# A fused attention and two-block kernel: the last block's first product as seven block products for two tiles of tokens at once

## The chip, the core and the metric

One core of a Trainium2 chip runs the whole program in one launch. The metric is the time of one execution on the device in microseconds (us). The chip's engines are named as in the profile: PE is TensorE's matmuls, PEld its weight loads, DVE is VectorE, ACT is ScalarE, POOL is GpSimd, SP is SyncE, which here only issues transfers.

## What is computed

Attention with pooled keys and values feeds a block that routes each token to one of eight experts, and a second, dense block follows. The change touches only the dense block:

```python
def _moe2_ref(x, w_in, w_out, g_ln):          # x: 4608 x 512, w_in: 512 x 1024, w_out: 1024 x 512
    h = x @ w_in
    e = np.exp(h - np.max(h, axis=-1, keepdims=True))
    solu = h * (e / (np.sum(e, axis=-1, keepdims=True) + 1e-09))
    mu = np.mean(solu, axis=-1, keepdims=True)
    var = np.mean((solu - mu) ** 2, axis=-1, keepdims=True)
    return ((solu - mu) / np.sqrt(var + 1e-06) * g_ln) @ w_out
```

## The kernel before

Tokens are worked on in 36 tiles of 128. Every float32 matrix product is done in float16 with each operand split into a high and a low part (the low part is what is left after rounding): high by high, high by low and low by high, so three matmuls for each 128 rows of the contraction. The split of a 128-row tile is a ScalarE copy into float16 (high) and a VectorE scalar_tensor_tensor (low, L119, L843, L849, L874, L1213). The tile of tokens is TensorE's stationary operand, so it must lie transposed; a DMA transpose issued by SyncE does that, in blocks of 128 x 128.

The program is ordered by hand: each engine's queue holds its instructions in the order in which the Python code emits them, and an instruction that waits holds up all that stand behind it on its engine.

The expert block runs expert by expert in eight tiles each (`body`). Weights of later stages are loaded, decoded and split between its groups of matmuls; lists called `works` hold these steps, and `body` takes one after each of its four groups of matmuls and one in the middle of the second product, and what is left over at its end, ahead of `fin`, which adds the tile's result and scatters it to `xres` with a GpSimd transfer. `d_load`, `d_decode`, `d_split` do that for `w_in` (i = 0 to 3) and `w_out` (4 to 7), in experts 5, 6 and 7 (`DP`). In the last expert `m_load` and `m_xt` also load, split and transpose the first three tiles of the dense block.

The dense block is the loop at the end. For tile i: `m_h` makes the first product in two halves of 512 columns, 12 matmuls each (L1159), and a maximum of each half (L1164). `m_soft` makes the exponential on ScalarE (L1181), the product with it and its sum on VectorE (L1185), and the sum of squares on ScalarE (L1188). `m_var` makes the reciprocal root: a power on GpSimd (L1198) between small VectorE operations. `m_norm` normalises on VectorE (L1207), splits (L1211, L1213) and transposes (L1212, L1214). `m_out` is the second product, 24 matmuls (L1222), its eviction on ScalarE (L1225) and the store (L1226). The order within the loop:

```python
for i in range(NT + AHEAD):          # AHEAD = 3: m_out runs three tiles behind m_h
    m_load(i + 4); m_h(i, 0)
    m_xt(i + 3)                      # the input of the tile three ahead
    m_h(i, 1); m_soft(i)
    m_norm(i - 1)
    m_var(i)
    m_out(i - AHEAD)
```

(the conditions at the first and last tiles are left out here). The halves have three PSUM banks each, the second product two.

## Time and profile before

| | |
|---|---|
| Median of three runs | 983.17 us (981.6 to 995.12) |
| The profiled execution, its own time | 977.48 us |
| Its span in the profile | 975.8 us |
| TensorE, mean granted clock over the span | 0.952 of full speed |
| Busy: PE, DVE, ACT, POOL | 891.2, 626.8, 429.8, 297.9 us |
| Matmuls | 7,838 |

The profile is one execution recorded by the hardware. A busy engine is one with an instruction in it; matmuls are pipelined, so a matmul's row shows 379 ns while the next one starts 216 ns later. The chain of work is followed back from the last instruction, at each step to what released it. The stage windows give the busy time of every engine in a stretch of the span, and beside it the clock that TensorE was granted (1.00 is 2.4 GHz, 0.50 is 1.2 GHz) and the mean busy share of the 16 DMA engines.

### The profile page before, as it was taken

The page shows a single profiled execution, that of the slowest core. Times are in us where ns is not written, and L with a number is a line of the kernel's source. Part 1 is how long each engine was busy: PE and PEld are TensorE (multiplying, and loading weights), DVE is VectorE, ACT ScalarE, POOL GpSimd, SP SyncE. Part 2 cuts the span into 40 slices and gives each one's busy share as a digit, 9 for nine tenths or more (in the row PEclk, how much of TensorE's full clock was granted, in tenths as well). Part 3 has the DMA queues.
Part 4 walks back from the last instruction along what each step waited for, and adds up shares of the span by engine and source line. Part 5 has one row for each costly group of instructions (what it writes and reads, how often), then busy time and mean ns, then how long its engine had stood idle before and what let it go on. Part 6 is the DMA issues. An engine that isn't in the chain of part 4 may idle for free. (4 is left out here: it accounts for less than half of the span.)

```text
span 975.8 us, 20287 instructions
## 1 busy us (share of the span) xinstructions
PE 891.2 (91%) x7838; PEld 563.5 (58%) x7838; DVE 626.8 (64%) x1420; ACT 429.8 (44%) x1002; POOL 297.9 (31%) x255
## 2 busy tenths in 40 slices
...
GB/s 292 226 344 336 229 265 269 108 214 186 338 156 228 183 186 184 241 236 69 82 120 171 98 55 56 104 127 148 142 128 161 110 125 145 109 136 134 98 98 86
DMA packets 189309, 163.98 MB, mean 168 GB/s; under 512 B 137296, under 2 KB 145488, under 8 KB 188656
## 3 DMA queue, kind: packets, MB, share of 16 engines
...
q14 instruction: 61, 0.50, 0.2%
...
## 5 line engine op out<-in xcount | busy, mean ns | idle before, releaser
L1222 PE MATMUL po<-woh,zt 128*128 128x512 f16 x576 | 177.9, 381 | 2.0 <-ACT o L1225 2.0
L1159 PE MATMUL ph<-wih,xt 128*128 128x512 f16 x576 | 176.7, 379 | 1.0 <-DVEq L1130 1.0
L1222 PEld LDWEIGHTS <-zt 128*128 128x128 f16 x864 | 84.9, 98 | 105.4 <-issue 4.6
L1159 PEld LDWEIGHTS <-xt 128*128 128x128 f16 x864 | 84.5, 98 | 103.2 <-issue 1.5
L1198 POOL TENSOR_TENSOR rr<-va,mhalf 128x1 f32<-128x1 f32 x36 | 19.8, 550 | 343.1 <-DVE va L1197 343.1
L1181 ACT ACTIVATE wst<-ph,ng 128x512 f32<-128x512 f32 x72 | 48.9, 683 | 158.4 <-DVE ng L1177 146.2
L1222 PE MATMUL po<-wol,zt 128*128 128x512 f16 x288 | 109.8, 381 | 0.0
L1159 PE MATMUL ph<-wil,xt 128*128 128x512 f16 x288 | 109.2, 379 | 0.0
L938 PE MATMUL ph<-xt,wsb 128*128 128x128 f16 x1536 | 93.5, 223 | 9.9 <-PEq L1136 8.8
L942 ACT ACTIVATE hh<-ph 128x256 f16<-128x256 f32 x104 | 38.5, 381 | 144.3 <-PE ph L938 133.6
L938 PEld LDWEIGHTS <-wsb 128*128 128x128 f16 x1536 | 91.0, 100 | 15.4 <-issue 12.8
L950 PE MATMUL py<-wsb,hh 128*128 128x512 f16 x256 | 76.2, 379 | 0.5 <-ACT hh L942 0.5
L943 DVE SCALAR_TENSOR_TENSOR hl<-ph,hh 128x256 f16<-128x256 f32 x104 | 42.5, 419 | 48.8 <-ACT hh L942 47.9
L1213 DVE SCALAR_TENSOR_TENSOR zl<-wst,zh 128x1024 f16<-128x1024 f32 x36 | 44.1, 1225 | 45.3 <-ACT zh L1211 45.3
L938 PE MATMUL ph<-xt,wsa 128*128 128x128 f16 x960 | 60.8, 226 | 12.5 <-PEq L1136 7.1
L1185 DVE SCALAR_TENSOR_TENSOR wst<-ph,wst 128x512 f32<-128x512 f32 x72 | 49.0, 692 | 30.6 <-ACT wst L1181 30.6
...
L938 PEld LDWEIGHTS <-wsa 128*128 128x128 f16 x960 | 58.4, 102 | 16.4 <-issue 13.2
L505 PE MATMUL px<-vbh,ah 128*128 128x148 f16 (+1 forms) x320 | 51.6, 228 | 16.3 <-DVE lraw L538 11.6
L269 POOL TENSOR_TENSOR kv<-kv 128x1280 f32<-128x1280 f32 (+3 forms) x28 | 57.7, 2060 | 22.3 <-DMA kv<-in_k_dram 21.1
L950 PEld LDWEIGHTS <-hh 128*128 128x128 f16 x416 | 39.3, 99 | 42.4 <-ACT hh L942 1.8
L1164 DVE TENSOR_REDUCE mx<-ph 128x1 f32<-128x512 f32 x72 | 49.4, 686 | 21.0 <-PE ph L1159 20.9
...
## 6 DMA issues: line engine op xcount, KB each, us to landing
...
```

Source lines behind the costliest of these rows:

```text
L269: eng.tensor_tensor(x_[:, :, 0:r, :], x_[:, :, 0:r, :], x_[:, :, r:2 * r, :], ALU.add)
L505: T.matmul(hd[sl, a, h:h + x1 - x0, :], s_, w_[rw, c0 + x0:c0 + x1, :], start=(n == 0 and bl == 2 * a), stop=(n == 2 and bl == 2 * a + 2))
L938: T.matmul(o_, ww[:, kc * DF + fc * P:kc * DF + (fc + 1) * P], xt[s_][:, x0 + kc, :], start=(n == 0), stop=(n == 11))
L942: S.activation(hh[hb][:, sl], ph, AF.Relu)
L943: V.scalar_tensor_tensor(hl[hb][:, sl], ph, 0.0, hh[hb][:, sl], ALU.max, ALU.subtract)
L950: T.matmul(py[hb], xx[:, fc * P:(fc + 1) * P], ww[:, fc * DM:(fc + 1) * DM], start=(fc == 0 and n == 0), stop=(fc == NFC - 1 and n == 2))
L1159: T.matmul(ph, xt[:, xx, :], ww[:, ws], start=(n == 0), stop=(n == 11))
L1164: V.tensor_reduce(sx[i]["mx"][:, half:half + 1], ph, axis=AX.X, op=ALU.max)
L1181: S.activation(e_[:, o_], ph[a], AF.Exp, bias=ng, scale=CE, accum_out=s2[:, a:a + 1])
L1185: V.scalar_tensor_tensor(u_[:, o_], ph[a], 1.0, e_[:, o_], ALU.mult, ALU.mult, accum_out=su[:, a:a + 1])
L1213: V.scalar_tensor_tensor(zl, u_, SZ, zh, ALU.mult, ALU.subtract)
L1222: T.matmul(po, zt[:, xx, :], ww[:, ws], start=(fc == 0 and n == 0), stop=(fc == NFC - 1 and n == 2))
```

## The change

Two tiles of tokens, a and b, make a pair. Their rows of x are taken as a 2 by 2 block matrix (tile a and b by the left and right 256 columns), `w_in` as another (256 rows by 512 columns each), and the product's four blocks come from seven block products of 128 x 256 by 256 x 512, six matmuls each, in Strassen's form with few additions. The sums of the blocks of x (`m_sum`, four per pair) and of the weight (`b_sum`, four in all) are made on GpSimd, the seven additions of products on VectorE, one product is copied out by ScalarE (`c1`). `m_xt` splits and transposes 1,536 columns of x and 2,048 of sums for a pair, in two DMA transposes. Products 1 and 7 share one PSUM bank, each of the other five has one of its own. The result h now lies in SBUF, so that exponential, product and maximum are each one operation of 1,024 columns. `m_var` is wholly on GpSimd (seven operations of 128 x 1), and the normalisation moves from VectorE to ScalarE. `m_soft` is split: what follows the exponential (`m_solu`) runs in the next pair's iteration. The second product runs two pairs behind, in quarters between the seven products. Only pair 0 is loaded in the last expert; pair 1 is loaded, summed, split and transposed ahead of the loop, later ones inside the loop of the pair before. The decoded `w_in` stays in `raw` and is split as seven blocks in the last expert.

```diff
--- before.py
+++ after.py
 NTAB = 4
 LATE = 26
 NTL = 3
-AHEAD = 3
-NPRE = 3
+AHEAD = 2
...
-    wih, wil, woh, wol = (dp.tile([P, 4096], F16, name=n) for n in ("wih", "wil", "woh", "wol"))
+    woh, wol = (dp.tile([P, 4096], F16, name=n) for n in ("woh", "wol"))
+    raw = dp.tile([P, 4, 1024], I32, name="raw")
...
+    def d_steps(i):
+        return d_decode(i) + ([] if i < 4 else [lambda: d_split(i)]) + [lambda: d_next(i)]
...
+    NB = ("11", "21", "22", "T1", "T2", "T3", "T4")
+    def wblk(n, lo):
+        k_ = NB.index(n) + 7 * lo
+        return wset[0][k_ // 4][:, (k_ % 4) * 1024:(k_ % 4 + 1) * 1024].rearrange(
+            "p (c d) -> p c d", c=2)
...
+    rwf = raw.bitcast(F32)
+    bsrc = {f"{a + 1}{b + 1}": rwf[:, 2 * a:2 * a + 2, 512 * b:512 * b + 512]
+            for a in range(2) for b in range(2)}
+    for i in range(4):
+        bsrc[f"T{i + 1}"] = wst[4 + i].rearrange("p (c d) -> p c d", c=2)
+    def b_sum(n, x0, x1):
+        G.tensor_tensor(bsrc[n], bsrc[x0], bsrc[x1], ALU.subtract)
+    def b_split(n):
+        S.activation(wblk(n, 0), bsrc[n], AF.Copy, scale=SWI)
+        V.scalar_tensor_tensor(wblk(n, 1), bsrc[n], SWI, wblk(n, 0), ALU.mult, ALU.subtract)
+    b_steps = [lambda: b_sum("T1", "12", "11"), lambda: b_split("11"), lambda: b_split("21"),
+               lambda: b_sum("T2", "22", "T1"), lambda: b_split("22"), lambda: b_split("T1"),
+               lambda: b_sum("T3", "22", "12"), lambda: b_split("T2"),
+               lambda: b_sum("T4", "21", "T2"), lambda: b_split("T3"), lambda: b_split("T4")]
...
+    def m_load(j, a):
+        if j == 0:
+            t_ = xg[gset(E, a)]
+        else:
+            t_ = dst[j % 2].bitcast(F32)[:, a * DM:(a + 1) * DM]
+        (G if j == 0 else nc.sync).dma_start(t_, m_rows(xres[P:XROWS, :], 2 * j + a))
+        sx.setdefault(j, {})[a] = t_
+    def m_sum(j):
+        xa, xb = sx[j][0], sx[j][1]
+        l_, r_ = slice(0, 256), slice(256, 512)
+        s_ = wst[4 + j % 2].rearrange("p (k d) -> p k d", k=4)
+        G.tensor_tensor(s_[:, 0], xb[:, l_], xb[:, r_], ALU.add)
+        G.tensor_tensor(s_[:, 2], xa[:, l_], xb[:, l_], ALU.subtract)
+        G.tensor_tensor(s_[:, 1], s_[:, 0], xa[:, l_], ALU.subtract)
+        G.tensor_tensor(s_[:, 3], xa[:, r_], s_[:, 1], ALU.subtract)
+    def m_xt(j):
+        d = sx[j]
+        xa, xb = d[0], d[1]
+        if j == 0:
+            ha, hs, xta, xts = (wst[i].bitcast(F16) for i in range(4))
+        else:
+            h_, x_ = wset[1][2 + j % 2], wset[1][j % 2]
+            ha, hs, xta, xts = h_[:, 0:1536], h_[:, 2048:], x_[:, 0:1536], x_[:, 2048:]
+        ha, hs, xta, xts = ha[:, 0:1536], hs[:, 0:2048], xta[:, 0:1536], xts[:, 0:2048]
+        s_ = wst[4 + j % 2]
+        S.activation(ha[:, 0:512], xa, AF.Copy, scale=SX2)
+        V.scalar_tensor_tensor(ha[:, 768:1280], xa, SX2, ha[:, 0:512], ALU.mult, ALU.subtract)
+        S.activation(ha[:, 512:768], xb[:, 256:], AF.Copy, scale=SX2)
+        V.scalar_tensor_tensor(ha[:, 1280:], xb[:, 256:], SX2, ha[:, 512:768], ALU.mult,
+                               ALU.subtract)
+        S.activation(hs[:, 0:1024], s_, AF.Copy, scale=SX2)
+        V.scalar_tensor_tensor(hs[:, 1024:], s_, SX2, hs[:, 0:1024], ALU.mult, ALU.subtract)
+        xta, xts = (t_.rearrange("p (c t) -> p c t", t=P) for t_ in (xta, xts))
+        nc.sync.dma_start_transpose(xta, ha)
+        nc.sync.dma_start_transpose(xts, hs)
+        d["A"] = {n: (xta[:, 2 * k:2 * k + 2], xta[:, 6 + 2 * k:8 + 2 * k])
+                  for k, n in enumerate(("11", "12", "22"))}
+        d["A"] |= {f"S{k + 1}": (xts[:, 2 * k:2 * k + 2], xts[:, 8 + 2 * k:10 + 2 * k])
...
-        DP = {E - 3: (0, 1), E - 2: (2, 3), E - 1: (4, 5, 6, 7)}
+        DP = {E - 3: (0, 1), E - 2: (2, 3, 4), E - 1: (5, 6, 7)}
...
             for n, j in enumerate(DP.get(e, ())):
-                works[n if last else n + 1] += [lambda f_=f_, j=j: f_(j)
-                                                for f_ in (d_decode, d_split, d_next)]
+                works[n + 1] += d_steps(j)
+            if last:
+                works[0] += b_steps[:5]
+                works[1] += b_steps[5:]
...
             if last:
-                m_load(0)
-                works[1].append(lambda: m_xt(0))
-                for i in range(1, NPRE):
-                    works[min(i + 1, nstatic - 1)] += (
-                        [lambda i=i: m_load(i)] + 3 * [lambda: None] + [lambda i=i: m_xt(i)])
+                m_load(0, 0)
+                works[2] += [lambda: m_load(0, 1)]
+                works[3] += [lambda: m_sum(0), lambda: None, lambda: m_xt(0)]
...
-        def m_h(i, half):
...
-            ph = pp.tile([P, 512], F32, tag=f"ph2{half}", name=f"ph2{half}", bufs=AHEAD)
-            n = 0
-            for kc in range(NKC):
-                ws = slice(kc * DF + half * 512, kc * DF + half * 512 + 512)
-                for xx, ww in ((kc, wih), (kc, wil), (NKC + kc, wih)):
-                    T.matmul(ph, xt[:, xx, :], ww[:, ws], start=(n == 0), stop=(n == 11))
-                    n += 1
...
-            V.tensor_reduce(sx[i]["mx"][:, half:half + 1], ph, axis=AX.X, op=ALU.max)
+        MM = {1: ("11", "11"), 2: ("12", "21"), 3: ("S4", "22"), 4: ("22", "T4"), 5: ("S1", "T1"),
+              6: ("S2", "T2"), 7: ("S3", "T3")}
+        def m_p(j, n):
+            bank = pp.tile([P, 512], F32, tag=f"b{n % 6}", name=f"b{n % 6}")
+            a, b = MM[n]
+            ah, al = sx[j]["A"][a]
+            k_ = 0
+            for c in range(2):
+                for xx, lo in ((ah, 0), (ah, 1), (al, 0)):
+                    T.matmul(bank, xx[:, c, :], wblk(b, lo)[:, c, :], start=(k_ == 0), stop=(k_ == 5))
+                    k_ += 1
+            return bank
...
         def m_soft(i):
...
-            d = sx[i]
-            ph = (d.pop(0), d.pop(1))
+            d = sx[i // 2, i % 2]
             def sm(nm, w=1):
                 d[nm] = fp.tile([P, w], F32, tag=nm, name=nm)
                 return d[nm]
-            mx, ng, s2, su = d["mx"], sm("ng2"), sm("s2_", 2), sm("su2", 2)
-            nm_, s_ = sm("nm2"), sm("ss2")
-            V.tensor_scalar(ng, mx[:, 0:1], mx[:, 1:2], -CE, ALU.max, ALU.mult)
+            d["sm"] = sm
+            mx, ng, s2 = sm("mx2"), sm("ng2"), sm("s2_")
+            V.tensor_reduce(mx, d["h"], axis=AX.X, op=ALU.max)
+            V.tensor_scalar(ng, mx, -CE, None, ALU.mult)
+            S.activation(wst[i % 2], d["h"], AF.Exp, bias=ng, scale=CE, accum_out=s2)
+        def m_solu(i):
+            d = sx[i // 2, i % 2]
+            sm = d.pop("sm")
+            su, nm_, s_ = sm("su2"), sm("nm2"), sm("ss2")
             e_, u_ = wst[i % 2], wst[2 + i % 2]
-            for a in range(2):
-                o_ = slice(a * 512, a * 512 + 512)
-                S.activation(e_[:, o_], ph[a], AF.Exp, bias=ng, scale=CE,
-                             accum_out=s2[:, a:a + 1])
-            for a in range(2):
-                o_ = slice(a * 512, a * 512 + 512)
-                V.scalar_tensor_tensor(u_[:, o_], ph[a], 1.0, e_[:, o_], ALU.mult, ALU.mult,
-                                       accum_out=su[:, a:a + 1])
-            V.tensor_scalar(nm_, su[:, 0:1], su[:, 1:2], -1.0 / DF, ALU.add, ALU.mult)
+            V.scalar_tensor_tensor(u_, d.pop("h"), 1.0, e_, ALU.mult, ALU.mult, accum_out=su)
+            V.tensor_scalar(nm_, su, -1.0 / DF, None, ALU.mult)
             S.activation(e_, u_, AF.Square, bias=nm_, accum_out=sm("sv2"))
-            V.tensor_scalar(s_, s2[:, 0:1], s2[:, 1:2], 1e-9, ALU.add, ALU.add)
+            V.tensor_scalar(s_, d["s2_"], 1e-9, None, ALU.add)
             V.scalar_tensor_tensor(s_, s_, EPS, s_, ALU.mult, ALU.mult)
         def m_var(i):
-            d = sx[i]
-            v_, r_, t_ = (fp.tile([P, 1], F32, tag=nm, name=nm) for nm in ("va2", "rr2", "tt2"))
-            d["r"] = r_
-            V.scalar_tensor_tensor(v_, d["sv2"], 1.0 / DF, d["ss2"], ALU.mult, ALU.add)
+            d = sx[i // 2, i % 2]
+            v_, r_, t_, nr_ = (fp.tile([P, 1], F32, tag=nm, name=nm)
+                               for nm in ("va2", "rr2", "tt2", "nr2"))
+            d["r"], d["nr"] = r_, nr_
+            G.tensor_scalar(v_, d["sv2"], 1.0 / DF, d["ss2"], ALU.mult, ALU.add)
             G.tensor_tensor(r_, v_, mhalf, ALU.pow)
-            V.scalar_tensor_tensor(t_, r_, v_, r_, ALU.mult, ALU.mult)
-            V.tensor_scalar(t_, t_, -0.5, 1.5, ALU.mult, ALU.add)
-            V.tensor_tensor(r_, r_, t_, ALU.mult)
+            G.tensor_tensor(t_, r_, r_, ALU.mult)
+            G.tensor_tensor(t_, t_, v_, ALU.mult)
+            G.tensor_scalar(t_, t_, -0.5, 1.5, ALU.mult, ALU.add)
+            G.tensor_tensor(r_, r_, t_, ALU.mult)
+            G.tensor_tensor(nr_, r_, d["nm2"], ALU.mult)
         def m_norm(i):
-            d = sx[i]
+            d = sx[i // 2, i % 2]
             u_ = wst[2 + i % 2]
-            V.tensor_scalar(u_, u_, d["nm2"], d["r"], ALU.add, ALU.mult)
-            d["zt"] = zt = fp.tile([P, 2 * NFC, P], F16, tag="zt", name="zt", bufs=AHEAD + 1)
+            S.activation(u_, u_, AF.Identity, bias=d["nr"], scale=d["r"])
+            d["zt"] = zt = fp.tile([P, 2 * NFC, P], F16, tag="zt", name="zt", bufs=4)
             zh = fp.tile([P, DF], F16, tag="zh", name="zh")
             zl = fp.tile([P, DF], F16, tag="zl", name="zl")
             S.activation(zh, u_, AF.Copy, scale=SZ)
...
             V.scalar_tensor_tensor(zl, u_, SZ, zh, ALU.mult, ALU.subtract)
             nc.sync.dma_start_transpose(zt[:, NFC:], zl)
-        def m_out(i):
-            zt = sx.pop(i)["zt"]
-            po = pp.tile([P, 512], F32, tag="po", name="po", bufs=2)
-            for fc in range(NFC):
+        def m_out(i, part):
+            d = sx[i // 2, i % 2]
+            zt = d["zt"]
+            if part == 0:
+                d["po"] = pp.tile([P, 512], F32, tag="po", name="po", bufs=2)
+            po = d["po"]
+            for fc in range(4 * part, 4 * part + 4):
                 ws = slice(fc * DM, (fc + 1) * DM)
                 for n, (xx, ww) in enumerate(((fc, woh), (fc, wol), (NFC + fc, woh))):
                     T.matmul(po, zt[:, xx, :], ww[:, ws], start=(fc == 0 and n == 0),
                              stop=(fc == NFC - 1 and n == 2))
-            o_ = fp.tile([P, DM], F32, tag="o2", name="o2")
-            S.activation(o_, po, AF.Copy, scale=1.0 / (SZ * SWO))
-            nc.sync.dma_start(m_rows(out, i), o_)
+            if part == 1:
+                o_ = fp.tile([P, DM], F32, tag="o2", name="o2")
+                S.activation(o_, po, AF.Copy, scale=1.0 / (SZ * SWO))
+                nc.sync.dma_start(m_rows(out, i), o_)
...
-        for i in range(NPRE, 4):
-            m_load(i)
-        for i in range(NT + AHEAD):
-            if i + 4 < NT:
-                m_load(i + 4)
-            if i < NT:
-                m_h(i, 0)
-            if 1 <= i and i + 3 < NT:
-                m_xt(i + 3)
-            if i < NT:
-                m_h(i, 1)
-            if i < NT:
-                m_soft(i)
-            if i == 0:
-                m_xt(3)
-            if 4 <= i <= NT:
-                m_norm(i - 1)
-            if i < NT:
-                m_var(i)
-            if i <= 2:
-                m_norm(i)
-            if i >= AHEAD:
-                m_out(i - AHEAD)
+        NPAIR = NT // 2
+        def add(o_, x0, x1):
+            V.tensor_tensor(o_, x0, x1, ALU.add)
+        for a in range(2):
+            m_load(1, a)
+        m_sum(1)
+        m_xt(1)
+        for j in range(NPAIR + AHEAD):
+            now, prev, o_ = j < NPAIR, 1 <= j <= NPAIR, 2 * (j - AHEAD)
+            if now:
+                if j + 2 < NPAIR:
+                    for a in range(2):
+                        m_load(j + 2, a)
+                h = [fp.tile([P, DF], F32, tag=f"h{n}", name=f"h{n}") for n in range(2)]
+                for a in range(2):
+                    sx[j, a] = {"h": h[a]}
+                uc, c1 = (wst[6 + j % 2][:, n * 512:n * 512 + 512] for n in range(2))
+                ha, hb, hc, hd = (h[n // 2][:, n % 2 * 512:n % 2 * 512 + 512] for n in range(4))
+                S.copy(c1, m_p(j, 1))
+                p2, p6 = m_p(j, 2), m_p(j, 6)
+            if prev:
+                m_solu(2 * j - 2)
+            if now:
+                add(ha, p2, c1)
+                add(uc, p6, c1)
+            if o_ >= 0:
+                m_out(o_, 0)
+            if prev:
+                m_var(2 * j - 2)
+                m_solu(2 * j - 1)
+            if now:
+                p5 = m_p(j, 5)
+            if prev:
+                m_norm(2 * j - 2)
+                m_var(2 * j - 1)
+            if now:
+                add(hb, p5, uc)
+            if o_ >= 0:
+                m_out(o_, 1)
+            if now:
+                p7 = m_p(j, 7)
+                add(hc, p7, uc)
+                add(hd, p5, hc)
+            if prev:
+                m_norm(2 * j - 1)
+            if 1 <= j and j + 1 < NPAIR:
+                m_sum(j + 1)
+                m_xt(j + 1)
+            if o_ >= 0:
+                m_out(o_ + 1, 0)
+            if now:
+                add(hb, m_p(j, 3), hb)
+                m_soft(2 * j)
+                add(hc, m_p(j, 4), hc)
+            if o_ >= 0:
+                m_out(o_ + 1, 1)
+            if now:
+                m_soft(2 * j + 1)
```

## Rows read from the trace of the kernel before

**Rows 1.** The page, part 1: busy time, share of the span, number of instructions.
```profile
PE 891.2 (91%) x7838; PEld 563.5 (58%) x7838; DVE 626.8 (64%) x1420; ACT 429.8 (44%) x1002; POOL 297.9 (31%) x255
```

**Rows 2.** Chain of work that ended last: start us, duration us, what.
```profile
594.96 2.89 DMA xres<-yo,tbi
598.03 3.31 DMA x<-xres
...
638.47 7.03 PE po L1222 x24
645.49 5.18 PE ph L1159 x24
...
951.11 20.73 PE po L1222 x96
```

**Rows 3.** Stage windows of 5 and 50 us: from:to, length, each engine's busy time.
```profile
639.00:644.00 5.00, 5.00 (x17) 1.86 (x15) 4.01 (x13) 1.45 (x5) 0.00 (x0) 0.66 0.65 162
...
750.00:800.00 50.00, 50.00 (x233) 22.70 (x232) 32.06 (x85) 21.38 (x43) 2.75 (x5) 1.00 0.61 132
```

**Rows 4.** Timeline of TensorE: start, duration, instruction, idle time before and its releaser.
```profile
375.61 2.85 PE L938 MATMUL ph<-xt,wsa 128*128 128x128 f16 x48 [1.45 <-PEq L1136]
...
594.88 0.38 PE L1159 MATMUL ph<-wih,xt 128*128 128x512 f16 x1 [0.99 <-DVEq L1130]
...
638.47 0.38 PE L1222 MATMUL po<-woh,zt 128*128 128x512 f16 x1 [1.99 <-ACT o L1225]
```

**Rows 5.** Groups of instructions by form, VectorE: busy us, mean ns, idle before.
```profile
L1164 DVE TENSOR_REDUCE mx<-ph 128x1 f32<-128x512 f32 x72 | 49.4, 686 | 21.0 <-PE ph L1159 20.9
L1185 DVE SCALAR_TENSOR_TENSOR wst<-ph,wst 128x512 f32<-128x512 f32 x72 | 49.0, 692 | 30.6 <-ACT wst L1181 30.6
L1213 DVE SCALAR_TENSOR_TENSOR zl<-wst,zh 128x1024 f16<-128x1024 f32 x36 | 44.1, 1225 | 45.3 <-ACT zh L1211 45.3
...
L1207 DVE TENSOR_SCALAR wst<-wst,nm,rr 128x1024 f32<-128x1024 f32 x36 | 29.1, 807 | 0.1
L874 DVE SCALAR_TENSOR_TENSOR xhl<-x,xhl 128x512 f16<-128x512 f32 x33 | 22.5, 681 | 1.6 <-ACT xhl L873 1.6
```

**Rows 6.** The same groups, ScalarE.
```profile
L1188 ACT ACTIVATE wst<-wst,nm 128x1024 f32<-128x1024 f32 x36 | 41.4, 1149 | 38.7 <-DVE nm L1187 38.7
...
L1211 ACT ACTIVATE zh<-wst 128x1024 f16<-128x1024 f32 x36 | 37.5, 1042 | 10.8 <-DVE wst L1207 10.8
...
L1225 ACT ACTIVATE o<-po 128x512 f32<-128x512 f32 x36 | 20.8, 577 | 9.4 <-PE po L1222 9.2
L873 ACT ACTIVATE xhl<-x 128x512 f16<-128x512 f32 x33 | 20.3, 616 | 0.0
```

**Rows 7.** The same groups, GpSimd.
```profile
L1198 POOL TENSOR_TENSOR rr<-va,mhalf 128x1 f32<-128x1 f32 x36 | 19.8, 550 | 343.1 <-DVE va L1197 343.1
...
L269 POOL TENSOR_TENSOR kv<-kv 128x1024 f32<-128x1024 f32 x7 | 16.5, 2355 | 0.0
...
L276 POOL TENSOR_TENSOR s<-kv 128x256 f32<-128x256 f32 x7 | 5.7, 812 | 0.5
```

**Rows 8.** SyncE's timeline; DMA busy tenths, 606 to 613; issues (us to landing).
```profile
741.40 1.28 SPq L1214 DMA_TRANSPOSE zt<-zl  x1
...
DMA  0000000007999999500000000003199998000699
...
zt<-zh SPq DMA_TRANSPOSE x20, 3.2
...
xt<-xhl SPq DMA_TRANSPOSE x20, 3.7
```

**Rows 9.** Groups by form, VectorE: one 64x64 subtraction beside GpSimd's, and alone.
```profile
L339 DVE TENSOR_TENSOR vbl<-s,vbh 64x64 f16<-64x64 f32 x7 | 5.7, 813 | 0.2
...
L377 DVE TENSOR_TENSOR vbl<-s,vbh 64x64 f16<-64x64 f32 x1 | 0.2, 223 | 0.0
```

**Rows 10.** Groups by form, TensorE, last expert (504 to 594 us).
```profile
L950 PE MATMUL py<-wsb,hl 128*128 128x512 f16 x64 | 24.3, 380 | 0.8 <-DVE hl L943 0.8
```

66 lines of the change are left out of this document (25 added, 41 removed).

## The prediction

> **What bounds the kernel now.** I read the page first, then the chain of work that ended last. TensorE is busy 91% of the span [rows 1], but that is an average over stages. From 638 us to the end the chain is nothing but matmuls of the second block: 24 of the first product, 24 of the second, in turn [rows 2]. Its last piece is 96 matmuls in 20.73 us, so 0.216 us each and 5.18 us for 24. The stage windows say the same: in 750 to 800 us TensorE is busy 50.00 of 50 us at full clock, VectorE 32.06, ScalarE 21.38, GpSimd 2.75, the DMA engines 0.61 [rows 3]. So here time is matmuls times 0.216 us, and the change takes matmuls away where they are the bound.
>
> The block runs on TensorE from 594.88 to 971.84 us (951.11 + 20.73), 376.96 us. Its 36 x 48 = 1,728 matmuls need 373.2 us at that pace. The other 3.8 us are one stall of 1.99 us [rows 4] and a low clock behind it: the next 24 matmuls took 7.03 instead of 5.18 us [rows 2], with the granted clock at a mean of 0.66 [rows 3]. Two readings matter later: this stage has no startup bubble, because after 594.88 four tiles of the first product run one behind the other; and shorter idle times, 0.99 and 1.45 us [rows 4], have no such row of slow matmuls behind them.
>
> **What it removes.** A pair of tiles needed 2 x 24 matmuls for the first product; seven products of 6 need 42. That is 6 x 18 = 108 fewer, 23.3 us at 0.216. A pair of tiles goes from 20.73 to 90 x 0.216 = 19.43 us. This is the whole gain, and the page's 7,838 matmuls should become 7,730.
>
> **What it adds, per pair, by engine.** VectorE ran 32.06 us in 50, 13.3 per pair. It gets seven additions of 512 (0.69 each by the 512-wide rows, 4.8), 0.9 us of wider splits; it loses the normalisation (0.81 x 2), small operations (about 1.4), and some fixed costs: about 15 of 19.4 us [rows 3, 5]. ScalarE ran 8.9; the moved normalisation (2 x 1.15, by the Square row), a copy (0.57) and 768 more columns of splits (0.9) make 12 to 13 [rows 3, 6]. GpSimd gets two chains of seven 128x1 operations and four sums of 128x256. The power takes 0.55; the 128x256 sum 0.81 and the 128x1024 one 2.36 [rows 7], so 1.5 us for 768 columns and about 0.3 for a tiny one. A chain is 2.5 us (if each took 0.55: 3.9), the sums 3.2, together 8 to 11 us. No engine becomes the bound by its load. DMA: 60 transposed blocks of 128x128 instead of 48. One transpose of eight blocks keeps the engines at 9 tenths for seven or eight of forty slices of 7 us, 1.3 us, so 0.17 a block [rows 8]; 12 x 0.17 = 2 us more per pair, beside a share of 0.61: not the bound either.
>
> **What is late next: the order in a pair.** Before, a tile's transposed input was made three tiles ahead. Now the input of pair j+1 is made inside pair j, behind the normalisation of pair j-1. From the pair's first matmul, t = 0: the second product's first tile ends after 48 matmuls at 10.4; its eviction on ScalarE stands before the second normalisation, so 10.6 + 0.58 = 11.2; normalise 1.15, 12.3; high part 1.04, 13.4; low part on VectorE 1.22, 14.6 [rows 5, 6]. SyncE issues that transpose for 1.28 us, 15.9, and only then that of the new pair's x. Eight blocks land 3.2 to 3.7 us after issue [rows 8]; twelve have 4 x 0.17 more, 3.9 to 4.4, I take 4.2: 20.1. The next pair's first product waits for it, and TensorE is free at 19.43: a stall of 0.7. The sums' transpose (16 blocks, 2.7 us of data behind the other) lands at about 22.8; the third product wants it at 20.1 + 2.6 = 22.7, so 0.1 more. If landings scale better than I think, the pair takes 19.43, if the issue also grows with the blocks (1.28 to 1.9), 20.8.
>
> VectorE keeps up with that order: what stands ahead of the seventh product's two additions (two products with the exponential, three additions, one low part) is 6.6 us by [rows 5], and that product ends at 11.7.
>
> GpSimd's new work can also hold up VectorE. The same 64x64 subtraction, both inputs in SBUF, takes 0.813 us where GpSimd adds beside it and 0.223 where VectorE does the sums itself [rows 9]. In the loop the low part at 13.4 falls beside GpSimd's four sums of 0.81, and VectorE's product beside GpSimd's chains. Bounds per pair: 0 and 0.81; I take 0.3, for the meetings are partial. So the pair takes 20.2 + 0.3 = 20.5, not 19.43: 1.05 x 15 pairs (j = 2 to 16) = 16 us given back.
>
> The Trainium skill ("SBUF — State Buffer", section "SBUF: two separate sides") calls that port pair an exclusive lock: whichever of a GpSimd operation and a VectorE operation with two SBUF inputs starts first keeps it for the whole instruction, and the other blocks. By that rule every meeting costs what is left of the instruction, up to 1.22 us for GpSimd behind a low part; the pair would be nearer 21.3 than my 20.5, and the total 12 us higher. The sum above goes by rows 9.
>
> **The start.** Pair 0 lies ready; pair 1 can only be loaded when the last scatter has landed (594.96 + 2.89), and its load lands at 598.03 + 3.31 = 601.3 [rows 2]. Now its sums (GpSimd 3.2) end at 604.6 to 605, their high part at 606.1, and both stand on ScalarE ahead of the copy of pair 0's first product, which ends at 606.8. The seventh product uses that same bank. TensorE has done four products (24 matmuls) by 600.1: stall 6.7 us. VectorE then has the low part until 607.4, seven additions and two maxima of 1024 (1.2 each, a little under two of 512), where the additions run close behind one another (0.6): 614.7 with the small ones [rows 5]. Then pair 1's iteration has no second product to fill it, and pair 2's input lies behind both normalisations: two products with the exponential, 619.3; Square, 620.7; normalise, high and low part, 624.2; three additions, 626.1; second low part, 627.3; splits and issue 628.6; landed 632.5. TensorE is idle from about 621 to 632.5. Up to there it has done 84 matmuls (18.1 us) in 37.6: 19.5 us lost, where before lost nothing. Behind such a gap the low clock costs 1.85 once more [rows 2]. Bounds: 14 (shorter sums and landings) and 24.
>
> **The end.** The last pair's normalised rows land at about 32.2 after that pair's first matmul; the second product of the pair before ends at 29.8: 2.4 us, and perhaps half a clock drop, 0.9.
>
> **Last experts.** Four splits leave experts 5 and 6, seven splits (1.05 on ScalarE, 1.2 on VectorE) and four sums of 2.36 us on GpSimd come into the last one's first two tiles; decoding is cut into single steps. Today TensorE waits 0.8 us for VectorE there [rows 10]: gain at most about 1.5, loss at most some 3 where four splits stand at the end of the second tile. I take nothing; the 5 us of second matmuls in each tile cover them.
>
> **Sum.** After: 1,620 matmuls 349.9 + start 19.5 + clock 1.8 + loop 16 + end 3.3 = 390.5 us, before 376.96: +13.5. The profiled execution had a span of 975.8 in 977.48 us, so 991.0; the median of the runs shown is 5.7 above it, 983.17, and I forecast against that: 996.7, say 997.
>
> **Rivals.**
> - *The pair runs at matmul pace*: the x of pair j+1 lands by 19.4 (it needs 0.7 us less, and no hold-up by GpSimd). Start and end stay: +13.5 - 16 = -2.5, 981.
> - *The full saving*: the start too is covered. It needs the copy of pair 0's first product not to be queued behind pair 1, against the order in the code. Then -23.3 + 3: 963 or less, faster by over 2%. The block's clean start today speaks for it, the order against.
> - *Slower by over 2%*: hold-up at GpSimd's sums lengthens every pair. At 0.81 and more per pair (GpSimd's chains behind VectorE's two-input operations, so that the second normalisation starts at 12 instead of 11.2) the pair takes 21.3: +12 on the forecast, 1,009. It decides from 20.9 per pair on, since 15 x 0.4 = 6 lifts 997 to 1,003. Stalls that then reach 2 us bring the low clock each time, 1.85 x 15 = 28 more at most, 1,037.
> - *It doesn't do what it says*: excluded by the code, but the count of matmuls will tell.
>
> **Chances.** Forecast (pair at 20 to 20.9, 988 to 1,003) 0.44; matmul pace 0.20; full saving 0.06; slower rival 0.30. A measurement of this kernel can tell about 2%, 20 us, from no change. So faster 0.06, same 0.64, slower 0.30. The range takes the matmul-pace case with some luck in the start (14 instead of 19.5) and the slower rival with a few clock drops: 977 to 1,017.
>
> **What would show it.** 7,730 matmuls; chain pieces of 90 matmuls per 20.5 us with an idle time before each pair's first product, released by the transposed x; two gaps of some 7 and 11 us between 600 and 633; GpSimd busy 8 to 11 us per pair; VectorE low parts beside the sums longer than 1.22. Wrong if the gaps at the start are missing, if the first product of a pair never waits, or if it is another engine's order (copy, additions) that ends the waits.

## The result: 1.4% slower, and the profile after

| | before | after |
|---|---|---|
| Median of six runs each | 984.07 us | 998.49 us (992.77 to 1004.58) |
| Ratio, 95% interval | | 1.014 (1.0106 to 1.0173) |
| Profiled execution, own time | 977.48 us | 992.77 us |
| Its span | 975.8 us | 991.0 us |
| Last expert, its first matmul to the dense block's | 90.12 us | 97.20 us |
| Dense block | 376.96 us | 381.62 us |

The forecast was 997.0, range 977 to 1,017, and most of the chance on "within 2%". The total came out as forecast. Its terms did not, as the last two lines of the table show: the dense block lost 4.7 us where I had 13.5, and the last expert, for which I had taken nothing, lost 7.1. Every ratio here compares the fast runs of a kernel (those within 1.5% of its fastest) with those of the kernel before in the same batch, so it need not be the quotient of the medians beside it.

First the page of the changed kernel, part 1, the line that answers to [rows 1]:

```profile
PE 876.5 (88%) x7730; PEld 555.9 (56%) x7730; DVE 672.3 (68%) x1279; ACT 492.9 (50%) x1005; POOL 436.9 (44%) x546
```

7,730 matmuls, 108 fewer, as the code said. TensorE is 14.7 us less busy, and the span is 15.2 us longer: it stands idle about 30 us more.

Two windows, to be held against [rows 3]; the second is one pair of the loop from first matmul to first matmul:

```profile
639.00:644.00 5.00, 0.00 (x0) 0.00 (x0) 4.97 (x7) 1.06 (x1) 0.19 (x1) 0.50 0.98 192
...
745.87:765.67 19.80, 19.60 (x91) 8.74 (x91) 15.10 (x27) 12.65 (x19) 7.92 (x18) 1.00 0.65 155
```

In the first TensorE does nothing at all for 5 us and the granted clock is at its lower level, 0.50. In the second VectorE is busy 15.10 us (forecast about 15), ScalarE 12.65 (12 to 13), GpSimd 7.92 (8 to 11): the loads were well counted, and none of them is the bound.

TensorE's timeline, to be held against [rows 4]: start, duration, instruction, and in brackets the idle time before it with its releaser. The last expert's first matmul before the change (the first line), then in the changed kernel the same, the dense block's first, two waits behind it, and in the loop the last matmul of one pair and the next pair's first product:

```profile
504.76 2.85 PE L938 MATMUL ph<-xt,wsb 128*128 128x128 f16 x48 [0.58 <-PEq L1136]
...
508.39 4.48 PE L1005 MATMUL ph<-xt,wsb 128*128 128x128 f16 x48 [2.37 <-PEq L1203]
...
605.59 5.34 PE L1230 MATMUL b<-wsa,wst 128*128 128x512 f16 x24 [0.99 <-DVEq L1197]
617.95 5.88 PE L1230 MATMUL b<-wsa,wst 128*128 128x512 f16 x18 [7.02 <-ACT wst L1327]
645.14 5.95 PE L1230 MATMUL b<-wsa,wsb 128*128 128x512 f16 x18 [12.25 <-DMA wsb<-wsb]
...
685.89 0.38 PE L1297 MATMUL po<-woh,zt 128*128 128x512 f16 x1
686.33 4.06 PE L1230 MATMUL b<-wsa,wsb 128*128 128x512 f16 x18
```

The two gaps of the start are the ones forecast, with the releasers forecast: the copy of product 1 (7.02 us; I had 6.7) and the transposed input of the third pair (12.25; I had about 11.5). Behind each of them 18 matmuls take 5.88 and 5.95 instead of 4.06 us: the low clock. The loop's first products follow one another at 666.67, 686.33, 706.46 and so on to 945.05, so 19.88 us per pair over 14 pairs; matmul pace is 19.43 and I had 20.5.

One pair in detail, the one that begins at 745.87, from the timelines of ScalarE, VectorE, SyncE and TensorE. It is the chain that the prediction wrote out, step for step (line numbers are the changed kernel's: L1278 normalises, L1282 makes the high and L1284 the low part, L1309 is an addition of products, L1285 the low part's transpose, L936 and L937 are those of x and of its sums):

```profile
756.93 1.23 ACT L1278 ACTIVATE wst<-wst,nr,rr 128x1024 f32<-128x1024 f32 x1
758.20 1.06 ACT L1282 ACTIVATE zh<-wst 128x1024 f16<-128x1024 f32 x1
...
758.46 0.69 DVE L1309 TENSOR_TENSOR h<-b,h 128x512 f32<-128x512 f32 x1
759.29 1.37 DVE L1284 SCALAR_TENSOR_TENSOR zl<-wst,zh 128x1024 f16<-128x1024 f32 x1
...
760.68 1.25 SPq L1285 DMA_TRANSPOSE zt<-zl  x1
762.03 1.48 SPq L936 DMA_TRANSPOSE wsb<-wsb  x1
763.60 1.84 SPq L937 DMA_TRANSPOSE wsb<-wsb  x1
...
765.67 0.82 PE L1230 MATMUL b<-wsa,wsb 128*128 128x512 f16 x3 [0.20 <-DMA wsb<-wsb]
```

Second normalisation at +11.06 us (forecast 11.2), low part at +13.42 (13.4), x transpose issued at +16.16 (15.9), next first product at +19.80. The order held; the product that waits for the landing starts 3.64 us after the issue (3.4 to 3.8 in the loop, once 4.5), where I had 4.2. In eight of the pairs a wait of 0.15 to 1.13 us is shown before the first product, in the others none, though these too take about 19.7. The rows at 685.89 and 686.33 show why: the first product starts 0.44 us behind the matmul before it instead of 0.216, but that matmul is drawn 0.38 us long, so a wait of about 0.2 us leaves no idle time to show.

The last expert in the changed kernel, VectorE, GpSimd and TensorE:

```profile
514.92 3.26 DVE L881 SCALAR_TENSOR_TENSOR wsa<-raw,wsa 128x1024 f16<-128x1024 f32 x1 [0.25 <-ACT wsa L880]
518.44 3.04 DVE L881 SCALAR_TENSOR_TENSOR wsa<-raw,wsa 128x1024 f16<-128x1024 f32 x1
522.08 1.21 DVE L881 SCALAR_TENSOR_TENSOR wsa<-raw,wsa 128x1024 f16<-128x1024 f32 x1
...
531.59 6.20 DVE L851 SCALAR_TENSOR_TENSOR wol<-dcv,gln,woh 128x512 f16<-128x512 f32 x2 [0.46 <-ACT woh L850]
537.71 4.62 DVE L881 SCALAR_TENSOR_TENSOR wsa<-wst,wsa 128x1024 f16<-128x1024 f32 x4
...
514.75 2.35 POOL L877 TENSOR_TENSOR wst<-raw 128x1024 f32<-128x1024 f32 x1 [6.67 <-DVE xt L990]
517.18 3.22 POOL L877 TENSOR_TENSOR wst<-raw,wst 128x1024 f32<-128x1024 f32 x1
531.88 2.37 POOL L877 TENSOR_TENSOR wst<-raw 128x1024 f32<-128x1024 f32 x1
534.19 2.37 POOL L877 TENSOR_TENSOR wst<-raw,wst 128x1024 f32<-128x1024 f32 x1
...
543.98 2.72 PE L1005 MATMUL ph<-xt,wsb 128*128 128x128 f16 x24 [5.26 <-DVE hl L1010]
```

A block's low part takes 1.21 us alone and 3.26 and 3.04 while GpSimd makes the sums of w_in's blocks; two 512-wide low parts of `w_out` together take 6.20, of which the first has 5.54, until both sums are done. The four splits left over at the end of the second tile come on top (4.62 us), and TensorE waits 5.26 us for the low part of h (`hl`), which is queued behind all that on VectorE. Matmul by matmul against the kernel before, the last expert loses 5.6 us at this place, the low clock behind the wait included, 1.2 at the splits of the first tile, and 1.6 in its first 48 matmuls, which run at a low clock (4.48 instead of 2.85 us); 1.4 come back later.

The wait doesn't always have this form. Eight of the kernels traced here (the changed one, and those below that leave the last expert as it is) have the same code in it: it takes 95.1 to 97.3 us in them, so it loses 5.0 to 7.2 against the one trace of before, and 97.20 is at the upper end. TensorE waits 5.1 to 5.3 us at the second tile's end in all eight, but only in three of them does a low part of `w_out` wait out both sums. In three others, as in the run "the copy first" below, the sums start later, and VectorE stands idle for 3.3 us until the one that the next split needs is made and copied:

```profile
526.46 3.53 DVE L881 SCALAR_TENSOR_TENSOR wsa<-wst,wsa 128x1024 f16<-128x1024 f32 x2 [3.34 <-ACT wsa L880]
```

The profiled executions differ by 15.3 us: 3.6 before the last expert, 7.1 in it and 4.7 in the dense block, of which some 0.1 comes back behind it. The 3.6 can't be told from scatter: kernels whose code up to there is the same start their last expert at 498.7 to 515.6 us. So from here on experiments are compared by stages, and by ratios to the kernel before in runs of the same batch.

### The profile page after: what moved, and what is told of

It is laid out like the page before. It is cut to its first block, busy times and chain, and to the rows that moved or that the text cites. A ratio compares the mean times of both kernels' runs of the same rounds, so it can differ in the third digit from the quotient of the medians.

```text
span 991.0 us, 20317 instructions
## 1 busy us (share of the span) xinstructions
PE 876.5 (88%) x7730; PEld 555.9 (56%) x7730; DVE 672.3 (68%) x1279; ACT 492.9 (50%) x1005; POOL 436.9 (44%) x546
## 5 line engine op out<-in xcount | busy, mean ns | idle before, releaser
L1297 PE MATMUL po<-woh,zt 128*128 128x512 f16 x576 | 181.9, 379 | 1.5 <-DMA zt<-zl 0.8
L1230 PE MATMUL b<-wsa,wsb 128*128 128x512 f16 x714 | 166.8, 382 | 16.3 <-DMA wsb<-wsb 15.8
L1230 PEld LDWEIGHTS <-wsb 128*128 128x128 f16 x714 | 69.0, 99 | 106.0 <-DMA wsb<-wsb 24.1
L1005 PEld LDWEIGHTS <-wsb 128*128 128x128 f16 x1536 | 91.4, 100 | 23.4 <-issue 12.7
L1266 POOL TENSOR_SCALAR va<-sv,ss 128x1 f32<-128x1 f32 x36 | 10.6, 294 | 199.9 <-ACT wst L1256 187.0
L1284 DVE SCALAR_TENSOR_TENSOR zl<-wst,zh 128x1024 f16<-128x1024 f32 x36 | 46.7, 1297 | 65.2 <-ACT zh L1282 63.1
L1246 ACT ACTIVATE wst<-h,ng 128x1024 f32<-128x1024 f32 x36 | 41.4, 1149 | 78.5 <-DVE ng L1245 78.5
L979 POOL DMA_INDIRECT xg<-xbuf,tbi x39 | 48.1, 1233 | 54.2 <-DMA xg<-xbuf,tbi 29.6
L1005 PEld LDWEIGHTS <-wsa 128*128 128x128 f16 x960 | 57.7, 101 | 16.6 <-issue 13.4
L504 PEld LDWEIGHTS <-ah 128*128 128x128 f16 (+2 forms) x560 | 44.3, 110 | 29.9 <-issue 16.9
L1256 ACT ACTIVATE wst<-wst,nm 128x1024 f32<-128x1024 f32 x36 | 41.3, 1148 | 39.3 <-DVE ss L1257 39.3
L1021 DVE SCALAR_TENSOR_TENSOR yo<-py,tbe,xg 128x512 f32<-128x512 f32 x26 | 19.4, 746 | 52.4 <-PE py L1017 48.0
```

Source lines behind the costliest of these rows:

```text
L504: T.matmul(hd[sl, a, h:h + x1 - x0, :], s_, w_[rw, c0 + x0:c0 + x1, :], start=(n == 0 and bl == 2 * a), stop=(n == 2 and bl == 2 * a + 2))
L979: G.indirect_dma_start(out=xg[s_], out_offset=None, in_=xbuf, in_offset=bass.IndirectOffsetOnAxis(ap=idx, axis=0))
L1005: T.matmul(o_, ww[:, kc * DF + fc * P:kc * DF + (fc + 1) * P], xt[s_][:, x0 + kc, :], start=(n == 0), stop=(n == 11))
L1230: T.matmul(bank, xx[:, c, :], wblk(b, lo)[:, c, :], start=(k_ == 0), stop=(k_ == 5))
L1246: S.activation(wst[i % 2], d["h"], AF.Exp, bias=ng, scale=CE, accum_out=s2)
L1256: S.activation(e_, u_, AF.Square, bias=nm_, accum_out=sm("sv2"))
```

## The experiments

The theory at this point: three separate losses, each of them of order and not of load. (1) In the last expert GpSimd's sums and VectorE's splits hold each other up, and they pile up at the end of a tile; (2) in the loop the next pair's input stands behind the normalisations of the pair before; (3) at the start the copy stands behind pair 1's input and pair 2's input behind pair 0's normalisations. The rival to each is that the new work itself costs what was lost, or that what one place gives back is lost at the next.

### The last expert: sums on VectorE

```diff
     def b_sum(n, x0, x1):
-        G.tensor_tensor(bsrc[n], bsrc[x0], bsrc[x1], ALU.subtract)
+        V.tensor_tensor(bsrc[n], bsrc[x0], bsrc[x1], ALU.subtract)
```

> The four sums of weight blocks are made on VectorE instead of GpSimd, all else as in the changed kernel. Theory (GpSimd's sums and VectorE's two-input splits keep each other off SBUF): the splits of 1024 columns that took 3.26 and 3.04 us beside the sums take 1.21, the pair of 512-wide splits that took 6.20 us takes 1.4, TensorE's idle time of 5.26 us in the last expert goes, and the dense block begins 6 to 9 us earlier; ratio to before about 1.006. Rival (the mere load of seven splits at the ends of tiles): VectorE gets 4.9 us more work there, the splits stay long or the idle time stays, ratio 1.014 or more.

986.95 us, ratio 1.0023 (0.9974 to 1.0073). The last expert takes 92.86 us instead of 97.20 (95.1 to 97.3 in the eight kernels with the sums on GpSimd), so 4.3 us less at most, where I had expected 6 to 9; the ratio, known to 5 us either way, is too coarse to settle it. VectorE's and TensorE's timelines:

```profile
514.28 1.22 DVE L877 TENSOR_TENSOR wst<-raw 128x1024 f32<-128x1024 f32 x1
517.12 1.23 DVE L881 SCALAR_TENSOR_TENSOR wsa<-raw,wsa 128x1024 f16<-128x1024 f32 x1 [0.25 <-ACT wsa L880]
...
542.73 1.65 PE L1005 MATMUL ph<-xt,wsb 128*128 128x128 f16 x24 [3.06 <-DVE hl L1010]
```

The same splits take 1.22 us, so the 3.26 was GpSimd's company. VectorE has four more operations and is still done sooner. The 3.06 us that TensorE still waits are plain load: two sums and four splits, one behind the other on VectorE at one tile's end.

### The last expert: spread out

```diff
+            if e == E - 2:            # sums: handed to tiles 4 to 7 of expert 6, on GpSimd
+                for n in range(4):
+                    works[4 + n].append(b_sums[n])
             if last:                  # splits: (11, T1), 21, 22, -, T2, T3, T4 in tiles 0 to 6
-                works[0] += b_steps[:5]
-                works[1] += b_steps[5:]
+                for n, f_ in enumerate(b_splits):
+                    works[n] += f_
...
```

> The changed kernel, with the preparation of w_in's seven blocks spread out: the four sums stay on GpSimd but run one each in tiles 4 to 7 of expert 6, and the seven splits run in tiles 0 to 6 of expert 7 (two in the first, none in the fourth), instead of all within the last expert's first two tiles. Theory (the last expert lost 7.1 us because GpSimd's sums and VectorE's splits with two SBUF inputs stop one another, 3.26 instead of 1.21 us, and because splits piled up at the end of a tile): the last expert, first matmul to the dense block's first, comes back from 97.2 to 90 to 91 us (90.12 before the change), and no split takes over 1.5 us. Ratio to the kernel before about 1.007. Rival: it is the number of instructions more (PE's queue waits at the expert's start, low clock) and not where they stand; then 95 us or more. Where the sums in expert 6 meet its own low parts, up to 2 us go there.

988.69 us, ratio 1.0044 (1.0006 to 1.0081). TensorE's timeline, first matmuls of the last expert and of the dense block, then one split and one sum:

```profile
508.18 2.63 PE L1005 MATMUL ph<-xt,wsb 128*128 128x128 f16 x44 [3.34 <-PEq L1206]
...
596.92 5.34 PE L1233 MATMUL b<-wsa,wst 128*128 128x512 f16 x24 [0.99 <-DVEq L1200]
...
513.66 2.45 DVE L881 SCALAR_TENSOR_TENSOR wsa<-wst,wsa 128x1024 f16<-128x1024 f32 x1
511.69 3.34 POOL L877 TENSOR_TENSOR wst<-raw 128x1024 f32<-128x1024 f32 x1
```

88.74 us, 8.5 less than in the changed kernel's trace and 1.4 less than before the change: the 0.8 of [rows 10] is gone with it. (The two kernels at the end of this section, with the same code here, take 90.86 and 88.56.) The run didn't do quite what its text says. Expert 6 has only four full tiles of tokens in these data, so the steps handed to its tiles 4 to 7 run one behind the other at its end, from 506.93 to 518.32 us, most of that beside the last expert's first tile. There sums and splits still meet: two splits take 1.66 and 2.45 us (none over 1.5 was expected), two sums 3.3. But no wait of TensorE for `hl` is left. So neither the work nor the meeting as such cost the 7 us, but where they stood: at the end of a tile, with the next tile's `hl` queued behind them.

### The loop: the next pair's input first

```diff
             if now:
                 add(ha, p2, c1)
                 add(uc, p6, c1)
+            if EARLY(j) and j + 1 < NPAIR:               # EARLY = lambda j: j >= 2
+                m_sum(j + 1)
+                m_xt(j + 1)
...
-            if 1 <= j and j + 1 < NPAIR:
+            if 1 <= j and not EARLY(j) and j + 1 < NPAIR:
                 m_sum(j + 1)
                 m_xt(j + 1)
```

> From pair 2 on, the next pair's sums, splits and transposes stand right behind the first two additions of the pair instead of behind the second normalisation. Theory (the pair is held by the chain eviction, normalise, high part, low part, transpose of x): a pair takes 90 matmuls at 0.216 = 19.43 us instead of 19.9, no idle time before a pair's first product, 7 us less in all, ratio about 1.007. Rival (the helpers' own loop, or the copy and additions, hold the pair): 19.9 stays, or another wait appears in its place, ratio 1.014.

982.25 us, ratio 1.0068 (1.0021 to 1.0115). First products of the fourth and the last pair:

```profile
659.85 4.05 PE L1230 MATMUL b<-wsa,wsb 128*128 128x512 f16 x18
...
931.80 4.05 PE L1230 MATMUL b<-wsa,wsb 128*128 128x512 f16 x18
```

271.95 us in 14 pairs: 19.425 each, matmul pace, and not one idle time before a first product. The dense block falls from 381.6 to 375.3 us. Position alone held the loop.

### The loop: which step of the chain holds it

The prediction put the second normalisation behind the eviction of the first second-product tile. Here that eviction is emitted behind the normalisation:

```diff
             if part == 1:
+                d["ev"] = lambda: m_ev(i, po)   # m_ev: S.activation(o_, po, ...) and the store
...
             if prev:
                 m_norm(2 * j - 1)
+            if o_ >= 0:
+                sx[o_ // 2, 0]["ev"]()
...
```

> The changed kernel, with the eviction of a pair's first second-product row tile (ScalarE, 0.60 us) emitted behind the normalisation of the second tile instead of ahead of it; nothing else moves. My step 'the second normalisation waits for that eviction' says: in the changed kernel the eviction started 10.57 us after the pair's first matmul and the normalisation at 11.06. Without it the normalisation needs only GpSimd's chain (ended about 9.8), so everything down to the new pair's input is about 1.2 us earlier; 19.90 us per pair become 19.43, no idle time before a pair's first product, 13 x 0.47 = 6 us less, ratio to the changed kernel 0.994. Rival A: the normalisation isn't held by the eviction but by the chain on GpSimd or by VectorE's low part order; then the pair stays at 19.9 and the ratio to the kernel before stays at 1.014. Rival B: SyncE's queue of transposes is the bound (five issues of 1.25 to 1.84 us, one behind the other); then the x transpose is issued no more than 0.3 us earlier.

1,006.89 us, ratio 1.0243 (1.0171 to 1.0314): slower than the change, and neither rival had that. 285.27 us in the last 14 pairs, 20.38 each. The pair from 753.16:

```profile
763.02 1.24 ACT L1278 ACTIVATE wst<-wst,nr,rr 128x1024 f32<-128x1024 f32 x1 [0.18 <-POOL nr L1272]
...
765.75 0.69 DVE L1312 TENSOR_TENSOR h<-b,h 128x512 f32<-128x512 f32 x1
766.36 1.57 DVE L1284 SCALAR_TENSOR_TENSOR zl<-wst,zh 128x1024 f16<-128x1024 f32 x1
...
769.29 0.53 SPq L1305 DMA_DIRECT2D out_dram<-o  x1
769.91 1.46 SPq L936 DMA_TRANSPOSE wsb<-wsb  x1
```

The normalisation does start 1.2 us earlier, at +9.86, held by GpSimd's chain alone. But the low part stays at +13.20, because VectorE's two additions of the seventh product end only then: a second path, as long as the first. And the store now stands ahead of the x transpose in SyncE's queue, which goes from +16.16 to +16.75. The next run takes that store behind the x transposes as well; "the last but one experiment" in its expectation is the run above.

```diff
-                nc.sync.dma_start(m_rows(out, i), o_)          # in the eviction
...
             if 1 <= j and j + 1 < NPAIR:
                 m_sum(j + 1)
                 m_xt(j + 1)
+            if o_ >= 0:
+                sx[o_ // 2, 0]["st"]()                         # the store alone
...
```

> The last but one experiment's late eviction made a pair 20.37 us long instead of 19.90, though the second normalisation then started 9.86 us after the pair's first matmul instead of 11.06. Its rows: the second low part still started at 13.20 us (13.42 before), because VectorE does the seventh product's two additions first (11.9 to 13.3), and the output's store, now behind the normalised rows' transposes on SyncE, put the x transpose off from 16.16 to 16.75. Here the eviction stays late and its store goes behind the x transposes. Theory (eviction and VectorE's additions hold the low part alike, and the store cost the rest): the x transpose is issued at 16.0 to 16.2 us and the pair takes 19.8 to 19.9 us, no better than the changed kernel. Rival (my first reading, the eviction alone holds the chain): 19.43 now that the store is out of the way.

277.69 us in 14 pairs, 19.835 each (one run, 996.74 us): the theory's 19.8 to 19.9. The store was what the run before had lost, and the eviction alone was never the bound. The next also takes the low part ahead of those two additions:

```diff
                 p7 = m_p(j, 7)
+                if prev:
+                    m_norm(2 * j - 1)
                 add(hc, p7, uc)
                 add(hd, p5, hc)
-            if prev:
+            elif prev:
                 m_norm(2 * j - 1)
```

> As the run before it, and in addition VectorE's low part of the second normalised tile stands ahead of the seventh product's two additions. Theory: with both holds gone the low part starts near 12.2 us after the pair's first matmul, the normalised rows' transposes are issued by 15, the x transpose at 15.2 to 15.9, and the pair takes 19.43 to 19.6 us. Rival: SyncE's issues (five transposes of 1.25 to 1.84 us in a row) or the landing times hold it whatever the engines do: 19.9.

282.55 us in 14 pairs, 20.18 each (one run, 987.66 us): theory and rival both missed. The pair from 737.91:

```profile
750.80 1.73 DVE L1284 SCALAR_TENSOR_TENSOR zl<-wst,zh 128x1024 f16<-128x1024 f32 x1
753.16 0.69 DVE L1312 TENSOR_TENSOR h<-b,h 128x512 f32<-128x512 f32 x1
753.77 0.68 DVE L929 SCALAR_TENSOR_TENSOR wsb<-dst,wsb 128x512 f16<-128x512 f32 x1
...
754.82 1.27 SPq L936 DMA_TRANSPOSE wsb<-wsb  x1
```

The low part starts earlier, at +12.89, and takes 1.73 instead of 1.22 us, for it now falls on GpSimd's sums. The additions come behind it, and behind them x's own low parts; with them the x transpose waits, until +16.91, though SyncE has issued the normalised rows' transposes by +16.3. VectorE has the same five operations ahead of that transpose in whichever order they are put: the second tile's low part, two additions, two low parts of x. In the changed kernel's pair they end at +15.7, and SyncE is free of the normalised rows at +16.1. So there was no one step to relieve: two queues run out within 0.4 us of each other, and of the edits tried only taking the input out from behind both (the run before these three) gives the 0.46 us.

### The start: the copy first

```diff
-        m_sum(1)
-        m_xt(1)
         for j in range(NPAIR + AHEAD):
...
                 add(hd, p5, hc)
+            if j == 0:
+                m_sum(1)
+                m_xt(1)
```

> Pair 1's sums, splits and transposes stand behind pair 0's additions instead of ahead of the loop. Theory (the copy of pair 0's first product waits on ScalarE behind pair 1's input): the idle time of 7.0 us before the seventh product goes; TensorE then waits 2 to 5 us for pair 1's input instead; VectorE's additions no longer queue behind pair 1's splits, so pair 2 begins about 3 us earlier; ratio about 1.011. Rival (the seventh product waits for something else, or the loss is only handed on): first idle time stays, or pair 2 begins as late as now, ratio 1.014.

984.63 us, ratio 1.0066 (1.0018 to 1.0113). TensorE's waits at the start:

```profile
606.72 4.45 PE L1230 MATMUL b<-wsa,wsb 128*128 128x512 f16 x12 [3.67 <-DMA wsb<-wsb]
611.59 6.65 PE L1230 MATMUL b<-wsa,wsb 128*128 128x512 f16 x30 [0.42 <-DMA wsb<-wsb]
630.45 6.00 PE L1230 MATMUL b<-wsa,wsb 128*128 128x512 f16 x18 [12.21 <-DMA wsb<-wsb]
```

The 7.02 us for the copy are gone; pair 1's input, which can't be loaded before the last scatter has landed, takes back 4.09. Net 2.9 us, from 39.55 to 36.63 until the third pair's first product.

### The start: pair 2's input ahead of pair 0's normalisations

```diff
+            if j == 1:
+                m_sum(2)
+                m_xt(2)
             if prev:
                 m_solu(2 * j - 2)
...
-            if 1 <= j and j + 1 < NPAIR:
+            if 2 <= j and j + 1 < NPAIR:
                 m_sum(j + 1)
                 m_xt(j + 1)
```

> Pair 2's sums, splits and transposes stand ahead of pair 0's product with the exponential (in pair 1's iteration) instead of behind pair 0's and 1's normalisation. Theory (the idle time of 12.25 us before pair 2 is that queue on VectorE and ScalarE): pair 2's first product follows pair 1's last directly; TensorE then waits some 5 us for pair 0's normalised rows at its second product; 6 to 8 us less, ratio about 1.007. Rival (the start is bound by the normalisation chain itself): the same 12 us of idle time move to the second product, ratio 1.014.

990.23 us, ratio 1.012 (1.0057 to 1.0184), no gain. VectorE's and TensorE's timelines:

```profile
647.30 1.23 DVE L1284 SCALAR_TENSOR_TENSOR zl<-wst,zh 128x1024 f16<-128x1024 f32 x1 [4.11 <-ACT zh L1282]
648.44 1.28 DVE L1309 TENSOR_TENSOR h<-b,wst 128x512 f32<-128x512 f32 x2
...
649.78 5.93 PE L1230 MATMUL b<-wsa,wsb 128*128 128x512 f16 x18 [9.57 <-DVE h L1309]
```

The wait has a new releaser. Pair 2's input is there, but its first product needs the bank of pair 1's seventh, which is free when VectorE has added that product; the addition stands behind pair 0's low part, which waits 4.11 us for ScalarE's normalised rows. The same chain, met by another queue: 62.17 us until the fourth pair's first product, 61.08 in the changed kernel.

### The start: all that TensorE needs ahead of all that it doesn't

```diff
-        m_sum(1)
-        m_xt(1)
...
+            if j == 0:                       # behind pair 0's additions
+                m_sum(1)
+                m_xt(1)
+            if j == 1:                       # pair 1's last additions, then the normalisations
+                add(hb, m_p(j, 3), hb)
+                add(hc, m_p(j, 4), hc)
+                m_norm(0)
+                m_var(1)
+            if j == 2:                       # five block products ahead of the first m_out
+                m_out(0, 0)
+                m_out(0, 1)
...
+            if j == 0:                       # behind pair 0's exponentials
+                m_sum(2)
+                m_xt(2)
```

> The changed kernel with the dense block's start in another order; the loop from the fourth pair on is unchanged. Pair 1's input behind pair 0's seven products' additions; pair 2's input right behind pair 0's exponentials, so ahead of any normalisation; in pair 1 all seven additions ahead of the two normalisations; in the third pair the first second-product behind the fifth block product. Theory: the start was lost by order alone (copy behind pair 1's input, pair 2's input behind pair 0's normalisation, and, as the last start experiment showed, pair 1's additions behind it too). From the dense block's first matmul to the fourth pair's first product the changed kernel took 61.08 us; of this some 46 are matmuls at full clock. I expect 48 to 51: 3.7 us waiting for pair 1's input, 0 to 3 for pair 2's, 1 to 3 for the first normalised rows, no 12 us gap. Gain 10 to 13 us, ratio to the kernel before 1.002. Rival: the loss is in the length of the chain itself (exponential, product, square, power, normalise, split, transpose, 17 us from h to the transposed rows) and only moves: the second product of pair 0 waits as long as pair 2 did, 58 us or more.

995.38 us, ratio 1.0124 (1.0049 to 1.0199). From 611.23 to 667.34: 56.11 us, a gain of 5, not 10 to 13; the ratio, with its interval, doesn't show it. TensorE's timeline:

```profile
624.11 4.05 PE L1230 MATMUL b<-wsa,wsb 128*128 128x512 f16 x12 [3.66 <-DMA wsb<-wsb]
...
639.31 7.03 PE L1230 MATMUL b<-wsa,wsb 128*128 128x512 f16 x24 [2.32 <-DVE h L1309]
650.09 2.19 PE L1230 MATMUL b<-wsa,wsb 128*128 128x512 f16 x6 [3.75 <-ACT wst L1325]
```

The gap of 12 us is gone; what is left is again an order: pair 2's copy stands on ScalarE behind two exponentials, so its seventh product waits 3.75 us, and behind each of these three waits the matmuls are slow (12 in 4.05 us, 24 in 7.03, 6 in 2.19). On VectorE 3.19 us pass idle ahead of the low part of pair 1's sums, with pair 0's last additions and maxima queued behind it.

### All three together, and the start once more

The first of these two kernels joins the spread-out blocks, the input first in the loop, and the start above.

> The spread-out blocks of w_in, the reordered start and, in the loop, the input of the next pair ahead of the normalisations (from the third pair on), together. If the three losses are separate: 7 + 11 + 6 = 24 us below the changed kernel, about 974 on a median of 984 for the kernel before: ratio 0.990. Loop 19.43 per pair, last expert 90 to 91, dense block 360 to 364 us against 376.96 before the change and 381.6 after it. If they stand in for one another (what one edit takes away, the next one shows), ratio 1.00 or more.

975.61 us, ratio 0.9897 (0.9859 to 0.9935), with 0.990 forecast. Last expert 90.86 us, loop 19.425 per pair, dense block 370.0: less than the 376.96 before the change, though not the 360 to 364 I had named, for the start gave 5 of the 11 us. The dense block is 11.6 us shorter than in the changed kernel, against 6.3 and 5.1 for its two edits alone, so these losses are separate; the last expert gives 6.3. The second kernel also changes the start:

```diff
-                S.copy(c1, m_p(j, 1))
+                if j != 2:
+                    S.copy(c1, m_p(j, 1))
...
             if j == 0:
                 m_sum(1)
-                m_xt(1)
+                m_xt_part(1, 0)                       # x's own blocks, and their transpose
+                m_xt_part(1, 1)                       # high part of the sums
...
                 m_norm(0)
+                S.copy(wst[6][:, 512:1024], m_p(2, 1))  # pair 2's first product and its copy
                 m_var(1)
...
+                m_xt_part(1, 2)                       # low part and transpose, behind m_soft(0), m_soft(1)
                 m_sum(2)
                 m_xt(2)
```

> The kernel with all three cures, and the start once more in another order: pair 0's last two additions, maxima and exponentials ahead of the low part of pair 1's sums (VectorE stood idle 3.2 us there), and pair 2's first product and its copy ahead of the second normalisation (TensorE waited 3.75 to 5.9 us for that copy, queued behind two exponentials). Theory: the rest of the start's loss is still order; pair 0's chain comes 4 us earlier, the wait for the copy goes, and from the dense block's first matmul to the fourth pair's first product it takes 50 to 53 us instead of 56.05 (61.08 in the changed kernel): 3 to 6 us less, ratio to the kernel before 0.984 to 0.988. Rival: what is left is the length of the chain and the low clock behind each gap; then 55 us or more and 0.990 as before.

960.23 us, ratio 0.980 (0.9755 to 0.9846): the fastest kernel here, 2.0% under the one before the change (1.5 to 2.5). TensorE's timeline:

```profile
593.96 9.22 PE L1245 MATMUL b<-wsa,wst 128*128 128x512 f16 x42 [0.99 <-DVEq L1212]
606.86 2.76 PE L1245 MATMUL b<-wsa,wsb 128*128 128x512 f16 x12 [3.67 <-DMA wsb<-wsb]
612.61 16.03 PE L1245 MATMUL b<-wsa,wsb 128*128 128x512 f16 x60 [2.99 <-DMA wsb<-wsb]
...
643.45 1.89 PE L1245 MATMUL b<-wsa,wsb 128*128 128x512 f16 x8 [1.86 <-DVE h L1325]
```

From 593.96 to 643.45, 49.49 us (50 to 53 expected; 61.08 in the changed kernel). 174 matmuls at 0.216 are 37.6 of them; three waits, all named in the rows, are 8.5, and a low clock most of the rest: the 60 matmuls behind the wait of 2.99 us take 16.03 us, at a granted clock of 0.82, while the 12 behind the 3.67 us run at full pace. The dense block is at 363.54 us, 13.4 under that before the change: of the 23.3 us that 108 matmuls are worth, more than half is there, and the last expert, 88.56 us, is 1.6 under.

## Why the total was right and two steps were not

- **What it removes**: right. 7,730 matmuls, and a pair without waits takes 19.425 us (forecast 19.43).
- **What it adds**: right. VectorE 15.10, ScalarE 12.65, GpSimd 7.92 us per pair, none the bound. The small GpSimd operations, bounded by 0.3 and 0.55, take 0.19 to 0.27, the power 0.55 (in half of the chains one small one takes up to 1.2); three of a pair's sums take 0.72, the first 1.75.
- **What is late next, the order in a pair**: the mechanism was right and confirmed by taking it away (19.88 to 19.425). Mis-sized was the landing of twelve blocks, 3.64 us against 4.2, scaled up from eight blocks' 3.2 to 3.7 by 0.17 a block; the rows show next to no growth. Also mis-sized was GpSimd's hold-up of VectorE: 0.15 us on the second tile's low part (1.37 against 1.22, the same in every pair), not 0.3. So a pair gave back 0.46 us and not 1.05: some 7 us over the loop, not 16. Reading the eviction as the step that holds the chain was half the truth: the additions of product 7, which I had set aside as "keeping up", were as late; moving the eviction gained 0.05 (19.835), and moving both lost 0.3 (20.18).
- **The start**: right in both gaps and their releasers, near in their sizes, and right in what a low clock costs. The third pair's first product came 39.55 us after the block's start, where I had 37.6, so this term was some 2 us too low. I had the gap for pair 2's input end with its order, though: the experiments showed the same chain of pair 0 reach TensorE through two other queues in turn (VectorE's additions, then ScalarE's copy).
- **The end**: 3.3 us forecast, 1.5 shown (two waits of 0.69 and 0.80 in the second products of the last pair).
- **Last experts, "I take nothing"**: the step that failed, by 7.1 us (5.0 to 7.2 over eight traces). It rested on the 5 us of second matmuls in a tile covering the four splits at the second tile's end, and those were counted by their undisturbed price, 1.2 us. What stood there on VectorE was 10.8 us (6.20 + 4.62), the wait was 5.26, and the low clock behind it I had left out. Even with every operation at its undisturbed price and the sums on VectorE, 3.06 us of wait are left. The meeting of GpSimd and VectorE I had priced in the loop from [rows 9] and not here, where a sum takes 2.35 us and not 0.72. That row I had also misread: 0.81 is a mean of seven, of which three run in 0.22 to 0.25 us, as fast as alone, and four, beside GpSimd, in 0.50 to 1.67. The runs showed both parts: 4.3 us come back with the sums off GpSimd, 8.5 with the pile-up spread, each in one trace. How much of the 4.3 is the meeting and how much the splits' wait for late sums, no run separates.

So the sum was right by luck: a loop priced 9 us too high and a last expert priced 7 us too low cancel. The Trainium skill ("SBUF — State Buffer", section "SBUF: two separate sides") has the shared port as an exclusive lock that whichever of the two starts first holds for the whole instruction. In the last expert the rows agree with it to 0.15 us: the split at 514.92 waits for GpSimd's sum to end at 517.10, and 1.22 more is 518.32, against 518.18 shown; GpSimd's next sum waits for that and ends at 520.40, and the second split ends 1.1 later. The low part at 531.59 doesn't fit it: it is shown 0.29 us ahead of GpSimd's sum and yet ends behind both sums, in this trace and two others; no run here shows why. What I made of that rule was wrong: in the loop the long waits fall on GpSimd (its first sum takes 1.75 instead of 0.72 us), where nobody waits for it, and the 21.3 us per pair did not come.

What stays open: if the profiled executions stand for the medians, some 3 us of the medians' 14.4 lie in neither the last expert nor the dense block. They stand before, where executions of the same code scatter by more, and no run here settles them.
